# First batch's and left-over scores as F32 products of 64 rows, and a fixed order of the transition

## The chip, the cores and the metric

The kernel runs on one core of one Trainium2 chip. The metric is device time in microseconds (us) of one execution, the median of several runs. Engines: TensorE (PE: matmuls; PEld: its weight loads), VectorE (DVE), ScalarE (ACT), GpSimd (POOL), SyncE (SP, which here only issues DMAs). Every engine works through its own list in order and waits at semaphores.

## The reference, cut to what matters

Three layers on 2304 tokens: attention that keeps each query's 32 best scores, a two-layer MLP with a gate, and a layer in which each token goes to one of eight experts.

```python
# attention: B, H, S, D = 4, 8, 576, 64
scores = scale * np.matmul(q, k.transpose(0, 1, 3, 2))
kth = np.partition(scores, -32, axis=-1)[..., -32:-31]
scores = np.where(scores >= kth, scores, -1e9)
attn = softmax(scores)
x = np.matmul(attn, v)                          # -> (2304, 512)
# first MLP: w_in (512, 2048), w_out (2048, 512)
h = x @ w_in
x = (h * np.clip(h + 3.0, 0.0, 6.0) / 6.0) @ w_out
# routed layer: 8 experts, w1 (512, 1024), w2 (1024, 512)
logits = (x / norm(x)) @ (emb / norm(emb)).T / tau
e = argmax(logits); gate_w = softmax(logits)[e]
out = gate_w * (np.maximum(x @ w1[e], 0.0) @ w2[e])
```

## The kernel before, in words

**Numbers.** Matmuls run on F32 data in two ways. An F32R product takes a rounded operand in one pass; to keep the precision, each operand is split in a high part (a cast on ScalarE) and a low part (a subtraction on GpSimd or VectorE), and three products, or two with stacked operands, are summed. A plain F32 product needs no split and becomes two TensorE instructions.

**Units and steps.** The attention is cut into 72 units, 18 for each of the four batches. A tile unit ("t", b, t, p) is 128 queries of a pair of heads; with 576 keys each head gives a 128 x 576 block of scores. 576 is four tiles of 128 and 64 left over, so a left-over unit ("r", b, p) takes the last 64 queries of two pairs of heads, four heads in all. The order in a batch is tiles 0 and 1 (four units each), one left-over unit, tile 2, the other left-over unit, tile 3; in the last batch both left-over units stand behind tile 1.

The units pass through a software pipeline: in step i (76 of them) unit i gets its scores (`scores`, L397, in two halves g of 288 keys, each copied out by `take`, L400) and `pairs` (L409 to L413, VectorE, larger and smaller of two halves), unit i-1 its 32 maxima (`select`, L428 and L431, VectorE), unit i-2 the mask (`relu`, L442, ScalarE, and `mask`, L446, GpSimd), unit i-3 the exponential (L452) and the scaling by the inverse sum, unit i-4 its transposes (`turned`, L479, copied by `keep`, L484) and the product with v (`values`, L497, F32, left and right column halves in turn).

**Splitting q and k.** `prep` (L373) casts q, `need_k` (L322, L323) casts k twice, `lows` (L381) subtracts on GpSimd, and `ship` (L331) copies between partition halves by DMA, so that K holds the high and the low part of one head on 128 rows. A tile unit's half is then four F32R instructions (two heads, high and low q). A left-over unit's q goes into `zq`, a tile filled with zeros but for its columns, and its half is eight F32R instructions, summed onto one 128-row block.

**Work beside the attention.** In the same steps the first MLP's weights are prepared: 32 pieces are loaded (`w_load`, L220), turned from float64 words by VectorE (`w_one` L231, `w_two` L238), ScalarE (`w_round` L246, `w_hi` L259) and GpSimd (`w_add` L251, `w_low` L263), and their low parts are stored to DRAM (`w_store`, L267, lo_dram). They go through `wf`, a tile with three buffers. From step 12 the MLP runs too: an item is an eighth of the hidden width for 256 tokens, `s1` (L568, 24 instructions into bank_h), `gate` (L576), `swish` (L580), `large` (L584), `small` (L587), and one step later `s2` (L603, two halves). The steps in `PAUSE` start no item. `embed` computes the norms of the expert embeddings in five parts after steps 11, 12, 13, 14 and 16; part 2 is a product (L166) into a half of bank_a, which `values` uses as well, and part 3 a square root (L169).

**Order.** In the steps every engine's order is written out by hand: the names in FIRST (steps 0 to 11), MID (12 to 20) and THEN (21 on) are called one after another, and an engine gets its instructions in that order. Behind the steps a planner orders instructions by priority and estimated times; there the rest of the MLP runs, the last two groups of 128 tokens (left-over queries, groups 16 and 17) come last, `route` computes their logits, `choose` and `rank` the expert and the place of each token, `place` (L693) writes the token's number into a table. `ahead` has by then loaded the expert with the most tokens and its first two blocks of tokens; `stage1` (L963) and `stage2` (L976) are the expert's two matmuls, `tokens` (L812, L816) gathers and transposes rows, `split1` and `split2` (L796, L797) split weights.

## Time and profile before

| | before |
|---|---|
| median of 3 runs | 1116.71 us (1112.76 to 1118.89) |
| profiled execution | 1116.48 us |
| its span, first to last instruction | 1114.8 us |
| PE busy | 983.8 us, 88% |
| DVE busy | 775.3 us, 70% |
| ACT busy | 727.1 us, 65% |
| POOL busy | 646.6 us, 58% |
| mean granted clock of TensorE | 0.956 |

Busy time of TensorE counts an instruction from its start to the modelled end of its result, and instructions overlap; what one adds to a stream is the distance to the next start. The granted clock is the share of 2.4 GHz that TensorE was given; 0.5 would be 1.2 GHz throughout.

### The profile page before, as it was taken

To read this page: it belongs to the slowest core of one execution; us is meant where nothing else is said; L and a number is where in the kernel's file an instruction comes from. 1 tells how busy PE (TensorE), PEld (TensorE's weight loads), DVE (VectorE), ACT (ScalarE), POOL (GpSimd) and SP (SyncE) were. 2 spreads that over 40 slices of the span, in tenths; PEclk is the share of its full clock that TensorE was granted. 3 is DMA by queue.
4 is the path that set the end of the run, shared out by engine and by line. 5 is a ranking of instruction groups with operands and counts; after the bars stand their busy time and mean duration, and the time that the engine had idled before them with its cause. 6 is when DMAs were issued, how large, how long until landed. Compare 5 with 4: busy or idle time off the path is not lost.

```text
span 1114.8 us, 20782 instructions
## 1 busy us (share of the span) xinstructions
PE 983.8 (88%) x7172; PEld 861.7 (77%) x7172; DVE 775.3 (70%) x2345; ACT 727.1 (65%) x1469; POOL 646.6 (58%) x815
## 2 busy tenths in 40 slices
PE   2566658799999999999999999999989799999994
PEld 1345556689989789989788979889978688887883
DVE  4999878988898988898998799511244345444540
ACT  4798859888787878788887788632335244435541
POOL 5789868886676886677896677723221442113200
PEclk9967888899999999999999999999999899999997
DMA  6545656655334555343555324447680654345540
GB/s 185 170 148 168 215 186 199 206 186 189 115 116 130 148 172 190 113 133 115 158 183 170 126 73 142 126 160 206 188 283 23 195 195 157 130 168 173 196 163 20
DMA packets 90225, 176.11 MB, mean 158 GB/s; under 512 B 20477, under 2 KB 38032, under 8 KB 90111
## 3 DMA queue, kind: packets, MB, share of 16 engines
q1 hardware_dynamic: 85695, 164.90, 46.7%
q0 software_dynamic: 4416, 9.80, 2.6%
q8 instruction: 58, 0.95, 0.4%
q14 instruction: 56, 0.46, 0.1%
HBM read 150.86 MB, written 19.41 MB: 153 GB/s over the span
## 4 chain that ended last, share of the span: by engine, by line
PE 66%; DVE 12%; issue 7%; DMA 6%; ACT 5%; POOL 2%; SPq 1%; POOLq 0%; DVEq 0%; ACTq 0%
PE bank_h L568 17%; PE y L603 15%; PE ph L963 8%; PE po L976 7%; PE bank_a L497 6%; PE ps_sc L397 5%; PE bank_t L479 5%; DVE A L428 3%; DVE left L431 2%; DMA xg<-y_dram,idt 1%; DMA a<-in_moe_w_dram 1%; PE bank_t L640 1%; DVE wf L238 1%; DVE wf L231 1%; DMA lo_dram<-wf 1%
## 5 line engine op out<-in xcount | busy, mean ns | idle before, releaser
L446 POOL TENSOR_TENSOR s<-s,z 128x576 f32<-128x576 f32 x144 | 188.5, 1310 | 32.6 <-ACT z L442 31.2
L568 PE MATMUL bank_h<-xh,vh 128*128 128x256 f32 x576 | 170.7, 296 | 1.1 <-DVE u L580 1.1
L568 PE MATMUL bank_h<-xl,vh 128*128 128x256 f32 x576 | 164.5, 286 | 2.2 <-DVE xl L524 2.2
L568 PE MATMUL bank_h<-xh,lo 128*128 128x256 f32 x576 | 164.4, 285 | 0.0
L428 DVE MAX8 A<-left 128x8 f32<-128x288 f32 (+1 forms) x288 | 159.9, 597 | 0.0
L587 POOL TENSOR_TENSOR gl<-u,gh 128x512 fp32r<-128x512 f32 x72 | 94.6, 1314 | 93.0 <-ACT gh L584 91.9
L479 PE MATMUL bank_t<-ident,s 128*128 128x128 f32 x648 | 104.8, 288 | 35.9 <-ACT pt L484 30.9
L397 PE MATMUL ps_sc<-kst,qh 128*128 128x288 f32 x256 | 87.8, 356 | 44.9 <-DVE left L413 21.2
L580 DVE SCALAR_TENSOR_TENSOR u<-u,bank_h 128x512 f32<-128x512 f32 x72 | 49.3, 684 | 101.3 <-ACT u L576 99.8
L603 PE MATMUL y<-wh,gh 128*128 128x512 f32 x288 | 115.3, 402 | 0.0
L797 DVE TENSOR_TENSOR l<-a,h 128x1024 fp32r<-128x1024 f32 x64 | 77.9, 1242 | 53.5 <-ACT h L796 53.3
L479 PEld LDWEIGHTS bank_t<-ident,s 128*128 128x128 f32 x648 | 73.2, 145 | 54.0 <-ACT pt L484 36.0
L568 PEld LDWEIGHTS bank_h<-xh,vh 128*128 128x128 f32 x576 | 112.0, 195 | 3.0 <-DVE u L580 1.3
L568 PEld LDWEIGHTS bank_h<-xl,vh 128*128 128x128 f32 x576 | 112.1, 195 | 2.8 <-DVE xl L524 2.4
L603 PE MATMUL y<-lo,gh 128*128 128x512 f32 x288 | 113.2, 393 | 0.6 <-DMA lo<-lo_dram 0.6
L603 PE MATMUL y<-wh,gl 128*128 128x512 f32 x288 | 111.5, 391 | 2.5 <-POOL gl L587 2.5
L442 ACT ACTIVATE z<-s,nb 128x576 bf16<-128x576 f32 x144 | 111.8, 778 | 2.0 <-POOL nb L436 2.0
L452 ACT ACTIVATE s<-s,nb 128x576 f32<-128x576 f32 x144 | 112.3, 781 | 0.7 <-POOL s L446 0.6
L568 PEld LDWEIGHTS bank_h<-xh,lo 128*128 128x128 f32 x576 | 111.8, 194 | 0.1
L400 ACT COPY s<-ps_sc 128x576 f32<-128x576 f32 x144 | 92.4, 642 | 29.5 <-PE ps_sc L397 26.4
L497 PE MATMUL bank_a<-pt,vt 128*64 128x128 f32 (+1 forms) x1600 | 107.6, 289 | 0.7 <-DVE pos L678 0.7
L497 PEld LDWEIGHTS bank_a<-pt,vt 128*64 128x64 f32 x1600 | 89.7, 152 | 23.3 <-issue 8.0
(229 smaller groups left out, 2674.5 us busy)
## 6 DMA issues: line engine op xcount, KB each, us to landing
lo<-lo_dram SPq DMA_DIRECT2D x144, 512.0 KB, 4.1
a<-in_moe_w_dram SPq DMA_DIRECT2D x64, 512.0 KB, 9.9
qraw<-in_q_dram SPq DMA_DIRECT2D x64, 128.0 KB, 3.0
w<-in_moe_w_in_dram SPq DMA_DIRECT2D x16, 512.0 KB, 4.6
lo_dram<-wf SPq DMA_DIRECT2D x32, 256.0 KB, 2.8
w<-in_moe_w_out_dram SPq DMA_DIRECT2D x16, 512.0 KB, 4.7
vt<-in_v_dram SPq DMA_DIRECT2D x16, 320.0 KB, 3.2
kraw<-in_k_dram SPq DMA_DIRECT2D x32, 144.0 KB, 2.8
```

Of the source, the lines that this page charges most:

```text
L397: nc.tensor.matmul(ps[:, n, :HS], t, kk[:, HS * g:HS * g + HS], start=(o == 0), stop=(o == len(parts) - 1))
L400: nc.scalar.copy(sbuf[i % NS][:, :, HS * g:HS * g + HS], ps_[i][:, :, :HS])
L428: nc.vector.max(A[:, n, 8 * r:8 * r + 8], src[:, n, :w])
L442: nc.scalar.activation(zb_[n], tile_of(i, n), AF.Relu, bias=sel[i][1][:, n, 1:2], scale=-BIG)
L446: nc.gpsimd.tensor_tensor(s, s, zb_[n], op=ALU.subtract)
L452: nc.scalar.activation(s, s, AF.Exp, bias=sel[i][1][:, n, 0:1], scale=SCALE, accum_out=sums[i][:, n:n + 1])
L479: nc.tensor.transpose(pp[:, 128 * k:128 * k + 128], e[:, 128 * (3 * c + k):128 * (3 * c + k) + 128], ident)
L497: nc.tensor.matmul(av[64 * n:64 * n + 64, c0:c1], vt[:, k, 64 * n:64 * n + 64], pt[:, k + 5 * n if k < 4 else 4, c0:c1], start=(o == 0), s ...
L568: nc.tensor.matmul(ph[:, a, :], w, x[:, k, :], start=(k == 0 and n == 0), stop=(k == 3 and n == 2))
L587: nc.gpsimd.tensor_tensor(state[q][1], state.pop((q, "u")).rearrange("p (a n) -> p a n", a=2), state[q][0].bitcast(F32), op=ALU.subtract)
L603: nc.tensor.matmul(state["y"][o], x[:, a, c], w, start=(f == 0 and n == 0), stop=(f == 15 and n == 2))
L963: nc.tensor.matmul(ph, l[:, k, 128 * f:128 * f + 128], x[:, k, c0:c1], start=(n == 0), stop=(n == 11))
```

## The change

- `plain(u)` is true for every left-over unit and for the tile units of the first batch (PLAIN = 1). Such units keep q and k as loaded: no cast, no subtraction, no `ship`. Their scores are F32 products of 64 rows: head 0 on rows 0 to 63, head 1 on rows 64 to 127, and for a left-over unit each of two pairs of heads on 64 columns as well. `zq` and its zeros go. The first batch's k stays in the pool of the split k, the left-over units of later batches load k again.
- The last batch's units stand in the order of the others; PAUSE ends with 67, 71 instead of 66, 67.
- The lists FIRST, MID and THEN are new.
- `wf` has four buffers; the left-over units' output goes through it.
- `embed` follows steps 4 to 8, and its product goes to bank_h.
- The first loads: q of unit 0 is issued by ScalarE's queue, and the first weight piece is loaded right behind k.
- The end of the MLP: the last s2, the logits of groups 16 and 17, `choose`, `rank`, `stage1` of the first 256 tokens and `split2` of the first expert stand in a fixed order; the second expert's first weights are loaded ahead of them.

```diff
-PAUSE = (13, 17, 31, 35, 49, 53, 66, 67)
+PLAIN = 1
+PAUSE = (13, 17, 31, 35, 49, 53, 67, 71)
-FIRST = ("hi0 turn0 bend0 keep0 turn1 pick0 lows ship turn2 bend1 keep1 keep2 expo0 expo1 pick1 one0 round1 s10 hi1 s20 s21 score0 "
-         "low0 load_k values take0 load_q two0 mask0 guard round0 inverse s11 store0 pick2 pick3 mask1 gate aside low1 xh score1 "
-         "scale swish take1 large prep one1 two1 add0 bounds small add1 xl load0 load1 pairs store1 need_v")
+FIRST = ("turn0 hi0 pick0 need_v keep0 turn1 one0 expo0 low0 s10 keep1 turn2 hi1 keep2 lows s20 store0 expo1 round0 round1 s11 "
+         "load_q gate two0 guard ship one1 score0 pick1 load_k bend0 swish take0 values add0 load0 two1 inverse xh low1 scale "
+         "pick2 mask0 large score1 xl add1 small take1 pick3 pairs prep s21 store1 bend1 load1 bounds aside mask1")
-MID = ("lows s10 round0 expo0 hi0 turn0 turn1 one0 expo1 s11 gate two0 s20 pick0 low0 pick1 guard s21 bend0 ship keep0 score0 "
-       "load_k store0 keep1 turn2 add0 hi1 swish one1 take0 mask0 keep2 load_q inverse score1 large values round1 two1 take1 "
-       "pick2 aside bend1 load0 scale xh pick3 low1 small add1 mask1 need_v pairs xl prep load1 store1 bounds")
+MID = ("turn0 round0 lows keep0 s10 turn1 expo0 s11 load_q ship hi0 low0 turn2 expo1 score0 bend0 guard one0 gate load_k hi1 "
+       "pick0 two0 keep1 store0 s20 one1 pick1 mask0 add0 keep2 take0 two1 values bend1 inverse round1 pick2 add1 scale swish "
+       "load0 score1 low1 xh load1 store1 mask1 pick3 xl take1 bounds aside need_v large pairs prep small s21")
-THEN = ("lows turn0 pick0 expo0 keep0 turn1 expo1 s10 s11 ship bend0 turn2 score0 keep1 pick1 guard gate take0 keep2 inverse "
-        "mask0 swish scale large aside bend1 pick2 load_k s20 pick3 score1 take1 s21 values small prep mask1 pairs place xh "
-        "bounds load_q xl need_v")
+THEN = ("turn0 pick0 turn1 expo0 keep0 lows s10 s11 load_q expo1 guard keep1 pick1 turn2 ship score0 load_k bend0 gate mask0 "
+        "take0 keep2 inverse swish large scale small aside bend1 place pick2 s20 pick3 score1 take1 prep pairs s21 mask1 bounds "
+        "values xh xl need_v")
...
-            emb["pe"] = pe = half_a()
+            emb["pe"] = pe = bank_h
...
-        e["both"] = mp.tile([128, DM], F32, tag="wf", name="wf", bufs=3)
+        e["both"] = mp.tile([128, DM], F32, tag="wf", name="wf", bufs=4)
...
-        first, last = (r[1:], []) if b < B - 1 else ([], r[1:])
-        units += t[0] + t[1] + r[:1] + last + t[2] + first + t[3]
+        units += t[0] + t[1] + r[:1] + t[2] + r[1:] + t[3]
...
+    def plain(u):
+        return u[0] == "r" or u[1] < PLAIN
+
     def load_k(i):
-        if i >= NU or units[i][0] != "t":
+        if i >= NU:
+            return
+        if units[i][0] == "r":
+            _, b, p = units[i]
+            for a in range(2):
+                if b < PLAIN:
+                    rest_k[i, a] = kraws[b, p + a]
+                else:
+                    rest_k[i, a] = raw = lp.tile([128, S], F32, tag="kraw", name="kraw", bufs=2)
+                    for n in range(2):
+                        nc.sync.dma_start(out=raw[64 * n:64 * n + 64, :], in_=kt[b * H + 2 * (p + a) + n][64 * n:64 * n + 64, :])
             return
...
-            kraws[b, p] = raw = lp.tile([128, S], F32, tag="kraw", name="kraw", bufs=2)
+            if b < PLAIN:
+                kraws[b, p] = raw = kp.tile([128, S], F32, tag="k", name="kpl")
+            else:
+                kraws[b, p] = raw = lp.tile([128, S], F32, tag="kraw", name="kraw", bufs=2)
...
+        if plain(u):
+            w = 128 if u[0] == "t" else 64
+            for a in range(128 // w):
+                kk = kraws[u[1], u[3]] if u[0] == "t" else rest_k[i, a]
+                for n in range(2):
+                    d = slice(64 * n, 64 * n + 64)
+                    nc.tensor.matmul(ps[w * a:w * a + w, n, :HS], Q[u][d, w * a:w * a + w], kk[d, HS * g:HS * g + HS], start=True, stop=True)
+            return
         for n in range(2):
-            if u[0] == "t":
-                parts = [(K[u[1], 2 * u[3] + n], 128 * n)]
-            else:
-                parts = [(K[u[1], 2 * (u[2] + a) + n], 256 * n + 64 * a) for a in range(2)]
-            parts = [(kk, t[:, c:c + 128]) for kk, c in parts for t in Q[u]]
-            for o, (kk, t) in enumerate(parts):
-                nc.tensor.matmul(ps[:, n, :HS], t, kk[:, HS * g:HS * g + HS], start=(o == 0), stop=(o == len(parts) - 1))
+            for o, t in enumerate(Q[u]):
+                nc.tensor.matmul(ps[:, n, :HS], t[:, 128 * n:128 * n + 128], K[u[1], 2 * u[3] + n][:, HS * g:HS * g + HS], start=(o == 0), stop=(o == 1))
...
-        if i in (11, 12, 13, 14, 16):
-            embed((11, 12, 13, 14, 16).index(i))
+        if i in (4, 5, 6, 7, 8):
+            embed((4, 5, 6, 7, 8).index(i))
...
             load_k(0)
-            load_q(0)
+            load_q(0, nc.scalar)
+            w_load(0)
+            load_k(1)
             load_q(1)
-            prep(0)
-            lows()
-            load_k(1)
-            ship()
             load_q(2)
-            w_load(0)
-            prep(1)
-            lows()
...
-        while moe or last or side:
+        while moe or side:
...
+        with tc.manual_schedule():
+            for o in range(2):
+                last[6](last[0], o)
...
+            load1(1)
+            yts = []
+            for o, (t, g) in enumerate(finals):
+                pp = pps()
+                for k in range(4):
+                    nc.tensor.transpose(pp[:, k, :], t[:, 128 * k:128 * k + 128], ident)
+                yts.append(gp.tile([128, 4, 128], F32, tag="ob", name="ytl"))
+                nc.scalar.copy(yts[o], pp)
+                stage1(0, 0, 256, (o,))
+            for o, (t, g) in enumerate(finals):
+                p2 = half_a()[:, :E]
+                for k in range(4):
+                    nc.tensor.matmul(p2, yts[o][:, k, :], ent[:, k, :], start=(k == 0), stop=(k == 3))
+                nc.vector.tensor_copy(l_all[:, g, :], p2)
+                scored[0] += 1
+            choose()
+            for t, g in finals:
+                sq = gp.tile([128, DM], F32, tag="ob", name="sql")
+                nc.scalar.activation(sq, t, AF.Square, accum_out=ss_all[:, g:g + 1])
+            stage1(0, 0, 256, (2, 3))
+            rank()
+            stage1(0, 0, 256, (4,))
+            split2(0, range(5, 8), lambda f: stage1(0, 0, 256, (f,)))
         with tc.high_priority(offset=500):
-            stage1(0, 0, 256)
-        split2(0)
+            while spots:
+                place()
```

## Rows read from the trace of the kernel before

**Rows 1.** The page's slices of the span, 40 equal ones, busy tenths.

```profile
PE   2566658799999999999999999999989799999994
DVE  4999878988898988898998799511244345444540
```

**Rows 2.** Stages: length, busy us (instructions) per engine, granted clock, DMA share, GB/s.

```profile
28.00:112.00 84.00, 50.98 (x285) 38.91 (x285) 83.10 (x255) 72.53 (x148) 71.09 (x79) 0.80 0.52 161
112.00:224.00 112.00, 80.77 (x588) 69.20 (x588) 97.61 (x282) 91.42 (x185) 91.12 (x96) 0.83 0.64 202
224.00:700.00 476.00, 465.38 (x3878) 414.79 (x3876) 421.97 (x1479) 383.85 (x834) 353.71 (x500) 1.00 0.46 145
840.00:896.00 56.00, 47.09 (x297) 41.39 (x296) 23.77 (x64) 22.59 (x41) 18.63 (x20) 0.91 0.37 116
```

**Rows 3.** Timeline of the start (start, length, instruction), and the page's row for K's loads.

```profile
0.80 1.21 SPq L315 DMA_DIRECT2D kraw<-in_k_dram  x2
9.51 0.49 SPq L220 DMA_DIRECT2D w<-in_moe_w_in_dram  x1
10.16 0.58 PE L397 MATMUL ps_sc<-kst,qh 128*128 128x288 f32 x1 [10.16 <-DMA kst<-kraw]
11.73 0.64 ACT L400 COPY s<-ps_sc 128x576 f32<-128x576 f32 x1 [3.93 <-PE ps_sc L397]
14.18 0.43 DVE L231 TENSOR_SCALAR wf<-w 128x512 int32<-128x512 int32 x1 [13.24 <-DMA w<-in_moe_w_in_dram]
15.41 0.47 DVE L409 TENSOR_TENSOR ps_sc<-ps_sc,s 128x288 f32<-128x288 f32 x1
...
kraw<-in_k_dram SPq DMA_DIRECT2D x32, 144.0 KB, 2.8
```

**Rows 4.** Timeline of TensorE in a step at full clock.

```profile
299.84 1.31 PE L497 MATMUL bank_a<-pt,vt 128*64 128x128 f32 x20
301.08 0.88 PE L479 MATMUL bank_t<-ident,s 128*128 128x128 f32 x6
301.71 0.36 PE L568 MATMUL bank_h<-xh,vh 128*128 128x256 f32 x1
...
305.27 0.30 PE L397 MATMUL ps_sc<-kst,qh 128*128 128x288 f32 x1
305.40 0.29 PE L397 MATMUL ps_sc<-kst,ql 128*128 128x288 f32 x1
```

**Rows 5.** VectorE's waits from 100 to 226 us: total us, times, longest.

```profile
DVE wf L231 <- DMA lo_dram<-wf: 6.6, 4, 2.4
DVE u L580 <- ACT u L576: 5.2, 2, 5.0
```

**Rows 6.** Timeline around the norms' product.

```profile
151.25 1.85 PE L166 MATMUL bank_a<-sq,onesf 128*128 128x8 f32 x8 [8.85 <-DVE xl L524]
158.42 0.69 ACT L576 ACTIVATE u<-bank_h,half 128x512 f32<-128x512 f32 x1 [9.03 <-PE bank_h L568]
166.08 1.28 ACT L169 ACT_TABLE_LOAD   x1
```

**Rows 7.** The transition: timeline lines, and two lines of the chain (start, us, what).

```profile
844.42 0.40 PE L603 MATMUL y<-wh,gl 128*128 128x512 f32 x1
861.12 0.17 DVE L682 CAST rows<-de 128x2 int32<-128x2 f32 x1
874.30 1.11 PE L816 MATMUL pxt<-ident,xg 128*128 128x128 f32 x4 [5.44 <-DMA xg<-y_dram,idt]
877.36 0.90 PE L816 MATMUL pxt<-ident,xg 96*128 96x96 f32 x4 [1.94 <-DMA xg<-y_dram,idt]
878.83 0.77 PE L963 MATMUL ph<-xh__10004,h 128*128 128x224 f32 x2 [0.57 <-ACT xh__10004 L817]
...
850.10 2.84 PE ph L963 x24
878.83 5.32 PE ph L963 x24
```

**Rows 8.** One line of the code by its instructions: duration ns min/median/max.

```profile
L231 DVE TENSOR_SCALAR wf<-w x32: 409/553/1443, 14.2 to 207.1; 128x512 int32<-128x512 int32 x32
```

More of the change, by code (lines that the diff above doesn't have):

```diff
@@ L295, in layers @@
     sbuf = [wk.tile([128, 2, S], F32, name=f"s{i}") for i in range(NS)]
-    zq = [wk.tile([128, 448], F32R, name=f"zq{i}") for i in range(2)]
     left = wk.tile([128, 2, S], F32, name="left")
@@ L627, in r1 @@
         def r1():
-            sq = mp.tile([128, DM], F32, tag="wf", name="sqy", bufs=3)
+            sq = mp.tile([128, DM], F32, tag="wf", name="sqy", bufs=4)
             nc.scalar.activation(sq, ysb, AF.Square, accum_out=ss_all[:, g:g + 1])
@@ L834, in ahead @@
         load2(0)
+        expert(1)
     def step(i, last):
@@ L887, in layers @@
     if True:
-        for t in zq:
-            nc.gpsimd.memset(t.bitcast(F32), 0.0)
         last = None
@@ L928, in layers, with split2 @@
                 finish_rest()
-        if "w1" not in late:
-            at.close()
-            ahead()
-        assert done_groups[0] == NG and "order" in late
-        st.close()
-        hp = mb.enter_context(tc.tile_pool(name="hp", bufs=1))
-        tk = mb.enter_context(tc.tile_pool(name="tk", bufs=1))
-        wb = mb.enter_context(tc.tile_pool(name="wb", bufs=1))
-        gp = mb.enter_context(tc.tile_pool(name="gp", bufs=3))
-        px = mb.enter_context(tc.tile_pool(name="px", bufs=2, space=PSUM))
-        po_ = mb.enter_context(tc.tile_pool(name="po_", bufs=3, space=PSUM))
+        assert "w1" in late and done_groups[0] == NG - 2
         hs = {}
-        def split2(r):
+        def split2(r, then=(), f=None):
+            then = deque(then)
             a2 = ws2[r]
@@ L949, in split2, with stage1 @@
                 split(h2[:, k:k + 2, :], l2[:, k:k + 2, :], a2[:, k:k + 2, :])
+                if then:
+                    f(then.popleft())
             ws2[r] = (h2, l2)
-        def stage1(r, c0, c1):
+        def stage1(r, c0, c1, fs_=range(8)):
             xh_, xl_ = tok[r]
@@ L957, in stage1 @@
             hh, hl = hs[r]
-            for f in range(8):
+            for f in fs_:
                 ph = late["ph"].tile([128, 512], F32, tag="ph", name="ph2")[:, :c1 - c0]
@@ L1011, in layers @@
         nc.tensor.transpose(pg[:NG, :128], gt, ident)
-        gts = fs.tile([NG, 128], F32, tag="gts", name="gts")
+        gts = fs.tile([NG, 128], F32, tag="df", name="gts")
         nc.vector.tensor_copy(gts, pg[:NG, :128])
@@ L1021, in layers @@
             if then is not None:
-                load1(then)
+                if r:
+                    load1(then)
                 load2(then)
```

88 lines of the change are left out of this document (49 added, 39 removed).

## The prediction

> **What bounds the kernel now.** I read the slices of the span first, then the same stages with sums, then each stage's waits. The slices show three regimes [rows 1]: VectorE at nine tenths while TensorE climbs (to about 224 us), TensorE at nine tenths to the end, and a dip of TensorE near 820 to 880 us. The stage table [rows 2] prices them: from 28 to 112 us VectorE is busy 83.10 of 84 us and TensorE only 50.98 at a granted clock of 0.80; from 112 to 224 VectorE has 97.61 of 112, so 14.4 us are idle, with ScalarE at 91.42 and GpSimd at 91.12 close behind; from 224 to 700 TensorE has 465.38 of 476 at full clock. So a microsecond is worth something in four places: before VectorE's first work, in VectorE's idle time of 112 to 224, in TensorE's work behind 224, and in the dip. Elsewhere ScalarE and GpSimd work comes and goes free.
>
> The sums are made against the profiled execution, 1116.5 us (span 1114.8 and 1.7 around it); the median of the runs shown is 1116.7, the same within 0.02%.
>
> **The start.** Before, step 0's scores need q and k split into two parts: two ScalarE casts of K, GpSimd subtractions and a copy between partition halves, and the first product starts at 10.16 us. Its result is copied at 11.73, but VectorE gets its first work only at 14.18, when the first weight piece lands, issued at 9.51, 4.67 us earlier; the scores' pairs follow at 15.41 [rows 3]. After, K and q go straight to TensorE, q through ScalarE's own queue, which is idle then. SyncE issues K's two halves from 0.80 for 1.21 us; 2.8 us from issue to landing gives about 4.8. The first score part takes some 1.4 us at the half clock (twice the 0.7 us worked out below): 6.2. The weight piece is issued third, at 2.0, and lands at 6.7. ScalarE's rounding of it stands ahead of the copy (about 0.7), the copy takes 0.64 as at 11.73 [rows 3]: 8.0. Second part and copy, with 0.2 of passing on: 10.3. Pairs at 10.4 instead of 15.41: **-5.0**, and as VectorE then has no idle time up to 112 us, all of it carries. Bounds: -2 if the copies queue, -6 if the weight piece lands early.
>
> **Steps 1 to 11.** In these steps VectorE's own list is the same: the first batch's units lose GpSimd subtractions, ScalarE casts and copies on SyncE, all hidden behind VectorE. One thing can leak: the 409 ns weight shift L231 has a median of 553 and a maximum of 1443 ns [rows 8], beside GpSimd work in the profile. Fewer subtractions and another order change these meetings; an excess of 144 ns by the median, times the 19 pieces of these steps, is 2.7 us, and I take about half, **-1.5** (bounds -6 and +4: the order was rewritten and can meet worse).
>
> The scores themselves get dearer. A plain F32 product goes as two instructions: L497's 800 products are 1600 instructions. Twenty of them take 1.24 us, 62 ns each for 128 columns, with left and right column halves in turn; six F32 transposes take 0.63 us, 105 ns for 128 columns in one block [rows 4]. That is 0.48 or 0.82 ns per column, and an F32 product of 288 columns costs 0.28 or 0.47 us. An F32R instruction of 288 columns has a pitch of 0.13 [rows 4]. A tile unit's part goes from 4 x 0.13 = 0.52 to two products, 0.56 to 0.95; I take 0.7, near L497's row, since the two heads lie in different rows of the array but only the second half of one product can meet the first of the next. A left-over unit's part goes from 8 x 0.13 = 1.04 to 1.11 to 1.89; I take 1.2. No row here shows a product of 64 rows, so the lower ends reach down to four blocks at once, 0.47. At the half clock all of these double; the scores' way (two parts, two copies) is then 2 x (1.4 + 0.64) plus about 1.5 of waits, 5.6 us, inside the 7 to 8 us in which VectorE picks maxima between two units' pairs. Cost 0 here; if the cover goes, see the third rival.
>
> The Trainium skill, TensorEngine Tiling (Array Packing), Theoretical Speedup, says that a contraction of at most 64 rows can run up to twice as fast by row tiles; by that the parts would be 0.47 and, with columns halved too, 0.24. In Key Properties it says against the change that "changing tiling mode (not just tile) drains the TensorE". With 0.1 us a drain as an estimate, two per part, 12 parts in full steps would add 1.2 us. No row here shows either for row halves.
>
> **Steps 12 to 21.** Of VectorE's 14.4 idle us, two waits hold 11.8 [rows 5]. The first, 6.6 us, is L231 waiting for a store to lo_dram: three `wf` buffers turn over too fast; a fourth comes in, and store0 moves ahead of the next step's need. The second, 5.2, is `swish` behind `gate`: ScalarE stood 9.03 us for bank_h because TensorE stood 8.85 us at the norms' product L166, which had taken a half of bank_a that L524 had still to read [rows 6]. The product moves to step 6 and to bank_h, unused there; the wait has no successor. The square root's table load, 1.28 us, and the one back also leave a stage where ScalarE is full for step 7, where VectorE covers them. What is late next: with VectorE packed, 97.6 us of its work faces 91 on ScalarE and GpSimd (which lose some 1 us a step of casts and subtractions) and TensorE's 80.77 at a clock of 0.83. I take two thirds of 11.8, -7.9, and give back 0.9 for five tile units' parts (5 x 2 x 0.18, half on the path): **-7.0**. Bounds: -13 and +3, the latter if the new order makes waits as large as it removes.
>
> **From step 22.** The list THEN keeps TensorE's order word for word (turn, s1, turn2, score0, s20, score1, s21, values); only ScalarE's bend0 and the loads of K and q move, and q and K come earlier. So tile units cost the same. The left-over units at steps 26, 44 and 62 stand in full steps: 3 x 2 x 0.16 = +1.0; those at 31, 49 and 67 are in pauses, where TensorE has room. In the last batch one such unit moves from a full step to a pause: -2 x 0.52 = -1.0. Sum **0**, bounds -4.4 and +4.1 (six parts at 0.47 or at 1.89, with the same -1.0). The left-over units' K loads (four issues each) go to SyncE two steps ahead of use; behind them stand only loads with a step or more to spare.
>
> **The transition.** Before, the second layer's last matmul starts at 844.42; the places (`rows`) are known at 861.12, 16.5 us after its end; the gathered tokens reach TensorE at 874.30 after 5.44 us of idling, the next after 1.94 more, and 24 instructions of 224 columns then take 5.32 us, while 24 of 256 columns had taken 2.84 [rows 7]. The stage's clock is 0.91 [rows 2]. Idle 5.44 + 1.94 + 0.57 (the wait before 878.83) and 2.7 of half clock: 10.7 us to win. After, `rank` has a fixed place behind four blocks of stage1 (half of 2.84 each, 5.7) and the transposes and logits of two tiles, about 3: 9.5 us instead of 16.5, so tokens come 7 us earlier, and the same filling (rest of stage1, first stage2 blocks) covers them. Against it: the planner had put 2.6 us of stage1 into waits ahead of 844, which the fixed order keeps behind. **-8.0**, bounds 0 and -12.
>
> **Sum**: -5.0 - 1.5 - 7.0 + 0 - 8.0 = -21.5, so 1116.5 - 21.5 = **1095.0**.
>
> **Rivals.** (a) The freed waits return elsewhere: in 112 to 224 the three engines are within 7% of each other, so packing one shows the next; and the fixed transition only trades idle places. Then the start, a third of the middle and a third of the transition remain: -5.0 - 2.3 - 2.7 = -10, 1106.5. For it: the near-equal sums. Against it: L166's stall is one instruction's and has no substitute. (b) Nothing to be measured: the start's gain is eaten by left-over products that run one after another (+4.1) and the middle is even: 1115. (c) Slower: F32 products run one after another, 1.9 us a tile part at the half clock, and the scores' way, 2 x (1.9 + 0.64) + 1.5 = 6.6, plus any queueing on ScalarE passes the 7 to 8 us between pairs. It decides once a copy queues over 1 us. Each of 11 steps then loses about 2 us and each of six in the middle 1.5: +31; with +4.1 behind, -5.0 at the start, and a transition of -8.0: 1138. For it: ScalarE's list now puts copies behind casts of weights. Against it: TensorE busy only 50.98 of 84. (d) Products in different row halves run wholly at once: six left-over parts at 0.47 instead of 1.2, -4.4, and ten tile parts in the middle at 0.47 instead of 0.7, half of them on the path, -1.2: 1089.4. For it: L497's column halves come near two at once [rows 4]. Against it: the two instructions of one product follow each other in one block. It is the two-fold rule of the Trainium skill, TensorEngine Tiling (Array Packing), Theoretical Speedup.
>
> **How the numbers follow.** Forecast 0.50, (a) 0.22, (b) 0.08, (c) 0.10, (d) 0.10. About 0.5%, 5.6 us, is what a measurement of this kernel can tell from no change; the bounds are 1110.9 and 1122.1. Faster: the forecast and (d), all but 0.01, and nine tenths of (a): 0.79. Same: (b) and the rest: 0.10; slower: (c) with a little of (b): 0.11. The range reaches from the sum with the better ends of start, middle and transition (another -1, -6 and -4: 1084) and a part of (d)'s -5.6, to past (a) and (b): 1080 to 1117. It leaves out (c) and about as much at the low end.
>
> **What would show it.** Right: VectorE's first pairs near 10.4 us; no L231 wait on lo_dram and no L166 stall; a clock above 0.83 in the middle; steps from 22 on at the same pace; xg's transposes without a wait of several microseconds. Wrong: idle VectorE between 28 and 112 (scores late), ScalarE or GpSimd releasing VectorE for 10 us in the middle, score parts of 1.9 us at full clock, or `rank` still 16 us behind the last y.

## The result, and the profile after

The changed kernel takes 1087.99 us (median of 4 runs, 1084.72 to 1092.13), the kernel before 1117.8 beside it: ratio 0.9743, 95% interval 0.9695 to 0.9791. A second set of 5 runs gave 1091.64 and 0.9738 (0.9707 to 0.9769). The forecast was 1095.0. The execution profiled took 1086.53 us, its span is 1084.8.

The sum can be laid out by marks that both traces share: the first instruction on VectorE that works on a unit's scores (its pairs), and TensorE's last matmul of the first MLP (the last y).

| us | before | after | difference | forecast |
|---|---|---|---|---|
| first pairs of unit 0 | 15.41 | 10.08 | -5.33 | -5.0 |
| unit 0 to unit 11 | 107.54 | 103.85 | -3.69 | -1.5 |
| unit 11 to unit 21 | 119.04 | 104.37 | -14.67 | -7.0 |
| unit 21 to unit 71 | 459.63 | 459.41 | -0.22 | 0 |
| unit 71 to the last y | 142.80 | 138.71 | -4.09 | (transition) |
| last y to the end of the span | 270.34 | 268.34 | -2.00 | -8.0 |

So -23.7 us come before unit 21, ten more than forecast, and the rest, -6.3, behind it. The -8.0 was forecast for the transition as a whole, the last two rows together. The page's slices (PE and DVE, busy tenths of 40 equal parts) answer to [rows 1]: the same three regimes, the first one ending a slice earlier.

```profile
PE   3666777999999999999999999999989998999994
DVE  6999999888889988889988889411234353445540
```

The stage table (length, busy us with instructions per engine in the order PE, PEld, DVE, ACT, POOL, then granted clock, DMA share, GB/s) answers to [rows 2]. From 112 to 224 us VectorE is now busy 106.31 of 112 instead of 97.61, ScalarE and GpSimd 99 instead of 91, and TensorE's clock is 0.92 instead of 0.83: the stage is packed more densely, by all engines at once.

```profile
28.00:112.00 84.00, 57.46 (x322) 36.60 (x323) 82.32 (x273) 76.20 (x154) 67.22 (x76) 0.72 0.49 161
112.00:224.00 112.00, 93.30 (x732) 75.62 (x731) 106.31 (x330) 99.35 (x204) 99.76 (x118) 0.92 0.69 224
224.00:700.00 476.00, 464.34 (x3910) 405.50 (x3908) 413.89 (x1443) 377.33 (x819) 347.77 (x483) 1.00 0.50 147
840.00:896.00 56.00, 53.32 (x322) 46.24 (x321) 25.07 (x36) 23.79 (x39) 23.25 (x23) 1.00 0.51 174
```

The timeline of the start (start, length, instruction, and in brackets the idle time before it with what ended it) answers to [rows 3]. Products start at 3.87 instead of 10.16, the weight piece lands for VectorE at 6.80 (6.7 forecast), the second copy runs at 9.41, the pairs follow at 10.08 (10.4 forecast).

```profile
3.87 2.64 PE L411 MATMUL ps_sc<-kpl,qpl 64*128 64x288 f32 x4 [3.87 <-DMA qpl<-in_q_dram]
...
6.80 0.43 DVE L232 TENSOR_SCALAR wf<-w 128x512 int32<-128x512 int32 x1 [5.87 <-DMA w<-in_moe_w_in_dram]
...
9.41 0.64 ACT L418 COPY s<-ps_sc 128x576 f32<-128x576 f32 x1 [1.43 <-PE ps_sc L411]
10.08 0.47 DVE L427 TENSOR_TENSOR ps_sc<-ps_sc,s 128x288 f32<-128x288 f32 x1 [2.13 <-ACT s L418]
```

VectorE's waits from 112 to 224 us (total, times, longest) answer to [rows 5]. Both waits of before are gone, and none over 1.3 us has come.

```profile
DVE ps_sc L427 <- ACT s L418: 2.5, 3, 1.3
DVE sums L477 <- POOL sums L474: 1.7, 2, 1.2
DVE u L598 <- ACT u L594: 1.0, 1, 1.0
```

The same by marks, from unit 11's pairs to unit 21's, first before, then after, in the columns of the stage table: VectorE's busy time (the third engine) goes from 102.95 to 99.73 us. Its waits of more than 0.15 us in this stretch go from 15.4 to 4.2.

```profile
122.95:241.99 119.04, 91.64 (x678) 79.41 (x680) 102.95 (x309) 96.61 (x196) 97.23 (x114) 0.87 0.62 194
113.93:218.30 104.37, 85.67 (x662) 68.17 (x662) 99.73 (x305) 93.53 (x191) 93.70 (x111) 0.92 0.68 217
```

The transition, answering to [rows 7]: `rows` is written 13.07 us behind the start of the last y instead of 16.70, and TensorE's waits for gathered tokens there are 0.90 and 1.45 us instead of 5.44 and 1.94.

```profile
816.42 0.39 PE L621 MATMUL y<-wh,gl 128*128 128x512 f32 x1
829.49 0.17 DVE L706 CAST rows<-de 128x2 int32<-128x2 f32 x1
842.24 0.63 PE L843 MATMUL pxt<-ident,xg 128*128 128x128 f32 x4 [0.90 <-DMA xg<-y_dram,idt]
844.89 0.52 PE L843 MATMUL pxt<-ident,xg 96*128 96x96 f32 x4 [1.45 <-DMA xg<-y_dram,idt]
```

### The profile page after: what moved, and what is told of

Read it like the earlier page. It is cut to its first block, busy times and chain, and to the rows that moved or that the text cites. A ratio compares the mean times of both kernels' runs of the same rounds, so it can differ in the third digit from the quotient of the medians.

```text
span 1084.8 us, 20732 instructions
## 1 busy us (share of the span) xinstructions
PE 979.7 (90%) x7172; PEld 833.9 (77%) x7172; DVE 763.1 (70%) x2345; ACT 714.1 (66%) x1437; POOL 619.5 (57%) x785
## 5 line engine op out<-in xcount | busy, mean ns | idle before, releaser
L464 POOL TENSOR_TENSOR s<-s,z 128x576 f32<-128x576 f32 x144 | 185.7, 1290 | 43.4 <-ACT z L460 42.0
L621 PE MATMUL y<-wh,gh 128*128 128x512 f32 x288 | 118.0, 410 | 0.0
L515 PEld LDWEIGHTS bank_a<-pt,vt 128*64 128x64 f32 x1600 | 87.2, 147 | 39.3 <-ACT pt L502 15.5
L515 PE MATMUL bank_a<-pt,vt 128*64 128x128 f32 (+1 forms) x1600 | 104.8, 284 | 11.2 <-ACT pt L502 9.9
L418 ACT COPY s<-ps_sc 128x576 f32<-128x576 f32 x144 | 92.2, 641 | 23.1 <-PE ps_sc L411 11.6
L502 ACT COPY pt<-bank_t 128x384 f32<-128x384 f32 x216 | 101.6, 476 | 0.5 <-PE bank_t L497 0.5
```

What stands on the lines that cost most here:

```text
L418: nc.scalar.copy(sbuf[i % NS][:, :, HS * g:HS * g + HS], ps_[i][:, :, :HS])
L464: nc.gpsimd.tensor_tensor(s, s, zb_[n], op=ALU.subtract)
L502: nc.scalar.copy(pts[i][:, 3 * c:3 * c + 3, :].rearrange("p k n -> p (k n)"), tb_.pop((i, c))[:, :384])
L515: nc.tensor.matmul(av[64 * n:64 * n + 64, c0:c1], vt[:, k, 64 * n:64 * n + 64], pt[:, k + 5 * n if k < 4 else 4, c0:c1], start=(o == 0), s ...
L621: nc.tensor.matmul(state["y"][o], x[:, a, c], w, start=(f == 0 and n == 0), stop=(f == 15 and n == 2))
```

## The experiments

Theory after the result: the gain before unit 21 is made of three parts that each free VectorE (the norms moved, a fourth `wf` buffer, products that leave GpSimd and ScalarE lighter, together with the new lists), and the fixed transition gives the rest. Rivals: one part alone carries it; or the transition's gain is from elsewhere. All times are compared with the kernel before on the same chip. The stretch behind the last y turned out to differ by up to 15 us between executions of one and the same kernel, so the table also gives the start of the last y, which is free of it. Where a mark is compared with after's below, it is with the mean of after and after_again (103.2, 105.0 and 816.8). The marks have a spread of their own: after, after_again, old_tail, xg3, load1_late and old_tail_xg3 have the same steps, and their profiles give 102.3 to 103.9, 102.6 to 105.7 and 812.7 to 817.2. The kernel before has one profile.

| kernel | median us | ratio (95%) | unit 0 to 11 | 11 to 21 | last y at | last y to end |
|---|---|---|---|---|---|---|
| before | 1117.8 | 1 | 107.5 | 119.0 | 844.4 | 270.3 |
| after | 1088.0 | 0.9743 (0.9695 to 0.9791) | 103.9 | 104.4 | 816.4 | 268.3 |
| after_again | 1091.6 | 0.9738 (0.9707 to 0.9769) | 102.5 | 105.7 | 817.2 | 283.3 |
| norms_back | 1093.6 | 0.9777 (0.9746 to 0.9809) | 99.4 | 108.6 | 814.2 | 279.5 |
| wf3 | 1114.7 | 0.9969 (0.9951 to 0.9988) | 109.9 | 115.6 | 835.2 | 274.5 |
| old_lists | 1105.8 | 0.9887 (0.9855 to 0.9919) | 110.6 | 108.1 | 826.7 | 277.1 |
| split_first | 1109.9 | 0.9924 (0.9899 to 0.9948) | 108.8 | 105.6 | 830.4 | 279.3 |
| same_rows | 1103.3 | 0.9861 (0.9828 to 0.9893) | 108.0 | 106.7 | 822.7 | 278.7 |
| old_tail | 1090.1 | 0.9745 (0.9713 to 0.9777) | 102.4 | 104.4 | 815.8 | 272.4 |
| before_norms | 1112.9 | 0.9947 (0.9929 to 0.9965) | 110.5 | 112.2 | 840.6 | 269.6 |
| before_norms_wf4 | 1109.7 | 0.9923 (0.9897 to 0.9949) | 110.7 | 106.8 | 835.9 | 272.4 |
| xg3 | 1089.1 | 0.9747 (0.9704 to 0.9790) | 102.3 | 104.7 | 814.6 | 269.3 |
| load1_late | 1093.4 | 0.9793 (0.9765 to 0.9822) | 102.7 | 102.6 | 812.7 | 273.0 |
| old_tail_xg3 | 1091.5 | 0.9767 (0.9743 to 0.9790) | 102.5 | 104.5 | 816.7 | 274.3 |

**The norms (norms_back, before_norms).** The one puts them back in the changed kernel, the other moves them in the kernel before.

```diff
 # norms_back
-            emb["pe"] = pe = bank_h
+            emb["pe"] = pe = half_a()
...
-        if i in (4, 5, 6, 7, 8):
-            embed((4, 5, 6, 7, 8).index(i))
+        if i in (11, 12, 13, 14, 16):
+            embed((11, 12, 13, 14, 16).index(i))
```

> The changed kernel with the norms of the expert embeddings back after steps 11, 12, 13, 14 and 16 and their product in a half of bank_a. If the stall of the product was worth what the prediction gave it (5.2 us of VectorE's waits, and the two table loads back among the full steps), steps 12 to 21 take 4 to 7 us more and the whole about 1093 us. If the new lists read that half of bank_a early enough (the product with v now stands before swish), no stall comes back and only the table loads cost: 0 to 2 us, about 1089 us.

> The kernel before with one part of the change alone: the norms of the embeddings after steps 4 to 8, their product into bank_h. Theory (my prediction's: the product's stall of 2.3 us and the square root's wait in the middle stood on VectorE's path, and the earlier steps have room): steps 11 to 21 shorten by 2 to 4 us, steps 0 to 11 grow by less than 2, the time is 1113 to 1117 against 1118. Rival (from the run with the norms back at steps 11 to 16 under the new lists, where steps 0 to 11 were 4.4 us shorter and 11 to 21 4.3 longer: the norms cost about 4 us wherever they stand): steps 0 to 11 grow by 4, 11 to 21 shrink by 4, no change in time within 2 us.

In the kernel before, the move takes 6.9 us out of units 11 to 21 and puts 3.0 into 0 to 11; the last y comes 3.8 earlier and the ratio is 0.9947. The middle wins more than the 4 us that either expectation allowed, and the steps ahead lose more than the theory's 2. So this part was undervalued in the middle (its wait is 5.2) and not free ahead of it: VectorE, the full engine there, does the norms' own three instructions, 2.2 us in before_norms. In the changed kernel no gain of the move can be told, though the middle answers nearly as the first expectation has it: 0 to 11 loses 3.8, 11 to 21 wins 3.6, the last y, 2.7 later than in norms_back, lies within the spread, and the intervals of the two ratios overlap. The reason stands in the trace of norms_back: under the new lists the product waits 1.06 us at its old place, where it had waited 8.85 [rows 6].

```profile
132.53 1.03 PE L167 MATMUL bank_a<-sq,onesf 128*128 128x8 f32 x8 [1.06 <-DVE xl L542]
```

**The fourth buffer (wf3, before_norms_wf4).**

```diff
 # wf3: wf with three buffers, xq in a tile of its own
-        e["both"] = mp.tile([128, DM], F32, tag="wf", name="wf", bufs=4)
+        e["both"] = mp.tile([128, DM], F32, tag="wf", name="wf", bufs=3)
...
-            xq = mp.tile([128, DM], F32, tag="wf", name="xq", bufs=4)[:, :128].rearrange("d (a t) -> d a t", a=2)
+            xq = mp.tile([128, 2, 64], F32, tag="xq", name="xq", bufs=1)
```

> The changed kernel with three wf buffers instead of four, and the left-over output in a tile of its own as before. If the stores to lo_dram were the wait and the fourth buffer removed it, VectorE's L232 waits for them again and steps 5 to 21 take 4 to 7 us more: about 1093 us. If the new lists' earlier store is what removed it, nothing moves: 1087 to 1089 us.

> The kernel before with two parts of the change: the norms after steps 4 to 8 and the fourth buffer of wf (with the left-over units' output through it). The norms alone gave 1112.93 against 1119.06. In the changed kernel taking the fourth buffer away cost some 23 us. Theory (the buffer pays only together with the new lists and the lighter ScalarE and GpSimd, since the old lists were laid out for three): steps 0 to 21 are 0 to 6 us shorter than with the norms alone, 1107 to 1113. Rival (the buffer is worth its 23 us by itself, and is most of the change): 1090 to 1096.

Without the buffer the changed kernel loses nearly all, far more than the 4 to 7 us expected: the last y is 18.4 us later. VectorE's waits from 28 to 240 us name the store to lo_dram for 14.9 of them; for one more wait of the same tile, 5.2, the profile names nothing.

```profile
DVE wf L232 <- DMA lo_dram<-wf: 14.9, 10, 5.7
DVE wf L232 <- issue: 5.2, 1, 5.2
```

Put into the kernel before beside the norms, the buffer takes another 5.4 us out of units 11 to 21, within the 0 to 6 expected: the first row below, VectorE's waits of before_norms from 112 to 240 us, is missing in before_norms_wf4 (second fence), where none is longer than 1.2.

```profile
DVE wf L231 <- DMA lo_dram<-wf: 8.1, 3, 3.9
DVE ps_sc L409 <- ACT s L400: 1.2, 1, 1.2
```

```profile
DVE u L580 <- ACT u L576: 1.5, 3, 0.9
DVE ps_sc L409 <- ACT s L400: 1.2, 1, 1.2
```

So norms and buffer together bring units 11 to 21 from 119.0 to 106.8 with the old lists and the split products, 12.3 of the 14.7 us that the middle won. By the marks the buffer is worth 5 us under the old lists (the intervals of these two ratios overlap) and 18 under the new ones; why so much more there, no run shows.

**The lists and the unsplit first batch (old_lists, split_first).** old_lists is the changed kernel with FIRST, MID and THEN of before; split_first has

```diff
-PLAIN = 1
+PLAIN = 0
```

and the order of the first loads and casts of before.

> The changed kernel with the three lists FIRST, MID and THEN of the kernel before, all else as changed. If the gain of steps 1 to 21 (18.4 us between the pairs of unit 0 and of unit 21) comes from the removed waits and the removed casts and subtractions, most of it stays: about 1092 us, steps 12 to 21 at 106 to 110 us. If it comes from the order itself, steps 12 to 21 go back towards 115 us and the whole to 1100 us or more.

> The changed kernel with PLAIN = 0: the first batch's tile units are split again (casts, subtractions, copies between halves, four F32R instructions a part, and the old first loads); the left-over units stay plain. By the prediction the start gives back 5 us and steps 1 to 21 about 2 us: about 1095 us. If the casts and subtractions that fell away were what let ScalarE and GpSimd keep up in steps 12 to 21 (8 us more gained there than forecast), these steps give back 5 us or more beyond the start: about 1100 us.

split_first costs more than either time expected. old_lists comes out at the second of its two (1100 or more), but not by the middle, which is 3.1 us longer there and 0.6 in split_first. split_first gives back 7.1 us at the start (first pairs at 17.64). In units 0 to 11 old_lists loses 7.4 and split_first 5.6 us, where VectorE's list of work is the same and its waits are small (at most 2.5 us in sum behind the first pairs). What differs is how long two of its instructions take. The rows are VectorE's groups from unit 0's pairs to unit 11's (busy us, mean ns, idle before), first the kernel before, then after, old_lists and split_first:

```profile
L231 DVE TENSOR_SCALAR wf<-w 128x512 int32<-128x512 int32 x18 | 14.3, 794 | 0.0
L238 DVE SCALAR_TENSOR_TENSOR wf<-w,wf 128x512 int32<-128x512 int32 x18 | 13.6, 756 | 0.6
```

```profile
L239 DVE SCALAR_TENSOR_TENSOR wf<-w,wf 128x512 int32<-128x512 int32 x18 | 13.2, 732 | 0.4
L232 DVE TENSOR_SCALAR wf<-w 128x512 int32<-128x512 int32 x18 | 7.5, 419 | 1.4 <-DMA w<-in_moe_w_in_dram 1.4
```

```profile
L239 DVE SCALAR_TENSOR_TENSOR wf<-w,wf 128x512 int32<-128x512 int32 x18 | 16.4, 913 | 0.6
L232 DVE TENSOR_SCALAR wf<-w 128x512 int32<-128x512 int32 x18 | 12.8, 711 | 0.0
```

```profile
L239 DVE SCALAR_TENSOR_TENSOR wf<-w,wf 128x512 int32<-128x512 int32 x18 | 16.3, 904 | 0.4
L232 DVE TENSOR_SCALAR wf<-w 128x512 int32<-128x512 int32 x18 | 9.2, 511 | 1.6 <-DMA w<-in_moe_w_out_dram 1.6
```

The shift of a weight piece takes 419 ns on the mean after and 794 before, 18 times: 6.8 us. Both instructions together are 8.5 us longer in old_lists than after, and 4.8 in split_first. A long one stands beside a GpSimd instruction that had begun before it, and ends 0.3 us after that one has ended, as here before (VectorE's shift, then GpSimd's mask, which ends at 39.35; the shift ends at 39.64):

```profile
38.20 1.44 DVE L231 TENSOR_SCALAR wf<-w 128x512 int32<-128x512 int32 x1
...
38.07 1.28 POOL L446 TENSOR_TENSOR s<-s,z 128x576 f32<-128x576 f32 x1
```

Of the 32 shifts of before, the 14 longest, 920 to 1443 ns, all stand so and end 0.28 to 0.29 us behind it; the four with no GpSimd instruction beside them take 420 to 427. So it is a wait inside the instruction, and no view of waits shows it. The Trainium skill, SBUF — State Buffer (Who interferes with whom), says that a tensor_scalar can run in a mode that uses the pair of ports which VectorE shares with GpSimd, and that the engine that issues first holds the pair for its whole instruction; the traces agree, with the lengths above. Under the new lists none of the 18 shifts begins with more than 0.16 us of a GpSimd instruction still to run, and they take 410 to 434 ns; with the split products GpSimd has 12 instructions more in the same eleven units (96 against 84), and shifts up to 877 ns are back. That both are needed follows from the two runs: before_norms needs 110.5 us for these units, before_norms_wf4 110.7 and after 103.2, and with either undone all or most of these 7 us are back.

**Products side by side (same_rows).** The first batch's two heads both stand on rows 0 to 63, q in two column ranges and k in two tiles; its left-over units load k again. Of the edit, the products:

```diff
+        if plain(u) and u[0] == "t":
+            for n in range(2):
+                nc.tensor.matmul(ps[:, n, :HS], Q[u][0:64, 128 * n:128 * n + 128], kraws[u[1], u[3]][n][0:64, HS * g:HS * g + HS], start=True, stop=True)
+            return
         if plain(u):
```

> The first batch's two heads both stand on rows 0 to 63 (q in two column ranges, k in two tiles, the same bytes and scores), so their two F32 products share one block of rows and cannot run side by side. Theory (the two products of a tile part overlap because they stand in different row halves): a tile part takes 0.95 to 1.0 us at full clock instead of 0.69, and about 1.9 instead of 1.3 at the lower clock. Over steps 0 to 20 with 16 units of two parts that is 32 x 0.3 to 0.6 = 10 to 19 us of TensorE time; since VectorE and the copies set the pace there, I expect 0 to 4 us of it in the kernel's time (1088 to 1092), most of it at the first pairs (+1). Rival (c) of the prediction, that the scores' way decides when the products run one after another: +20 or more, first in steps 0 to 11, with waits of VectorE's pairs for ScalarE's copies.

TensorE's timeline at full clock, first after, then same_rows: a tile unit's part lasts 0.69 us to the next instruction's start in the one and 1.17 in the other; at the lower clock it is 1.26 (38.57 to 39.83) and 2.18 (38.78 to 40.96).

```profile
148.97 0.76 PE L411 MATMUL ps_sc<-kpl,qpl 64*128 64x288 f32 x4
149.66 0.50 PE L621 MATMUL y<-wh,gh 128*128 128x512 f32 x1
...
264.01 0.39 PE L621 MATMUL y<-lo,gh 128*128 128x512 f32 x1
264.24 0.39 PE L621 MATMUL y<-wh,gl 128*128 128x512 f32 x1
264.56 0.72 PE L411 MATMUL ps_sc<-kraw,qpl 64*64 64x288 f32 x8
265.21 0.50 PE L621 MATMUL y<-wh,gh 128*128 128x512 f32 x1
265.54 0.39 PE L621 MATMUL y<-lo,gh 128*128 128x512 f32 x1
265.77 0.40 PE L621 MATMUL y<-wh,gl 128*128 128x512 f32 x1
```

```profile
160.43 1.23 PE L406 MATMUL ps_sc<-kpl,qpl 64*128 64x288 f32 x4
161.60 0.50 PE L624 MATMUL y<-wh,gh 128*128 128x512 f32 x1
...
38.78 2.25 PE L406 MATMUL ps_sc<-kpl,qpl 64*128 64x288 f32 x4
40.96 0.48 PE L518 MATMUL bank_a<-pt,vt 128*64 128x128 f32 x2
```

So the two products of a part do run side by side. The lower rows of the first fence show a left-over unit's four products, on two halves of rows and of columns, in 0.65 us, less than two products need. In the raw starts all four blocks' first instructions begin within 0.02 us, and the second ones 0.29 later. The same rows show what the change of blocks costs: y's products start 0.23 us apart, the scores 0.32 behind one, and the first y product behind the scores takes 0.33 to the next start. That is some 0.1 us each way. Taking the side-by-side products away puts the last y 5.9 us later, more than the 0 to 4 expected and far from rival (c)'s 20, although TensorE's granted clock rose: 0.94 instead of 0.77 between unit 0 and unit 11, with TensorE busy 84.4 us instead of 64.9. VectorE's waits for copies of scores are 1.9 us there instead of 0.2 (without the one ahead of the first pairs), and 5.9 instead of 2.5 between units 11 and 21. The median is 11.6 us above after_again's; some 6 of them aren't in the marks, and behind the last y nothing was edited.

**The end of the MLP (old_tail, after_again).** old_tail is the changed kernel with the planner's end:

```diff
-            final = gs[o] >= NG - 2
+            final = False
...
-        while moe or side:
+        while moe or last or side:
...
-            load1(1)
-            yts = []
...
-            rank()
-            stage1(0, 0, 256, (4,))
-            split2(0, range(5, 8), lambda f: stage1(0, 0, 256, (f,)))
```

> The changed kernel with the end of the MLP as before: the planner orders the last logits, choose, rank, stage1 and split2, and the second expert's first weights are loaded late. Theory (the fixed order is what shortened the stretch behind step 71): rows are written about 16 us behind the last y instead of 13, the time is 4 to 8 us longer, 1092 to 1096. Rival (the stretch behind step 71 is shorter for another reason, such as the emptier queue of MLP items, and the fixed order only trades one wait for another): within 2 us of the changed kernel, 1087 to 1090.

> The changed kernel itself, once more, beside three others on one chip. The four experiments before it all ended with 274.5 to 279.5 us from the last y to the end, against 268.3 in the changed kernel's profile, with the same instructions in the same order on every engine there. If that is a cost of their edits, this run shows 268 to 270 and a time near 1088. If it differs from one execution to the next, by when the gathered rows arrive, this run may show 272 to 280 as well, and the four times then carry up to 10 us that are not their edits'.

The theory fell: 0.9745 against 0.9738 on the same chip. In old_tail `rows` is 16.91 us behind the last y, 3.84 later than after, as expected, and the waits for gathered tokens are back:

```profile
832.70 0.17 DVE L706 CAST rows<-de 128x2 int32<-128x2 f32 x1
...
846.30 1.12 PE L843 MATMUL pxt<-ident,xg 128*128 128x128 f32 x4 [5.86 <-DMA xg<-y_dram,idt]
850.26 0.90 PE L843 MATMUL pxt<-ident,xg 96*128 96x96 f32 x4 [2.84 <-DMA xg<-y_dram,idt]
```

But from `rows` to the end it needs 255.4 us, while the fixed order needs 255.3 in after and 270.4 in after_again. Over all profiles of the table the planner's order needs 252.9 to 257.3 us in five, the fixed order 255.3 to 270.4 in nine. So what the fixed order wins ahead of `rows` it gives back behind, in after itself least. The shorter stretch from unit 71 to the last y (138.79 in old_tail) isn't its doing either: 252 second-layer matmuls stand there before, 240 after and in old_tail, as the last batch's units and pauses were laid otherwise, and from unit 54 to unit 71 that batch takes 2.5 us longer for it.

**Where it is given back (xg3, load1_late, old_tail_xg3).**

```diff
 # xg3, and in old_tail_xg3 with old_tail's edits
-        pool("xg", bufs=2)
+        pool("xg", bufs=3)
 # load1_late: the second expert's first weights behind the table
-            load1(1)
             yts = []
...
         for r in TURNS[1:]:
             load_ids(r, 0, 4)
+        load1(1)
```

> The changed kernel with one more buffer for gathered rows of tokens (three instead of two). With the old, planner-ordered end the time was the same (1090.05 against 1091.64) although the rows were written 3.9 us later, so the fixed order's gain is given back behind them. Theory A: it is given back where TensorE waits for gathered rows (3.8 to 4.0 us about 100 us behind the last y in the executions of the fixed order, 0.5 to 1.1 in those of the planner's), since GpSimd issues these gathers only when TensorE has freed one of the two buffers. Then a third buffer takes 4 to 8 us off the stretch from the rows to the end (with the half clock that follows such a wait), and the time is 1082 to 1087. Theory B: the giving back has other causes (the second expert's weights, loaded 25 us earlier, beside the gathers): the wait stays or moves, within 2 us of the changed kernel, 1087 to 1092.

> The changed kernel with the second expert's first weights (2 MB) issued behind the rows' table, as in the kernel before, not ahead of the fixed order. Theory B: these loads stand beside the last y rows, the table and the first gathers, and move the later loads of weights too; without them there the stretch from the rows to the end is 253 to 256 us, as in the three executions of the planner's order, and the time is 1082 to 1087. Theory A (the buffers for gathered rows are what counts): within 2 us of the changed kernel, with the waits for gathered rows as they were, 1087 to 1092; a later load may even cost 1 to 3 us where its splitting stands on ScalarE's path.

> The planner-ordered end together with three buffers for gathered rows. Theory A: the planner's order waits for gathered rows 5.4 and 2.8 us ahead of the first expert's rest (about 24 and 31 us behind the last y), which is the latency from the table to the rows and not the buffers, so the third buffer gives 0 to 2 us: 1088 to 1091. Rival: any buffer shortens it, 1084 or less.

Theory A's wait is there in after and goes with the third buffer. These are TensorE's transposes of the next expert's rows, in after, then in xg3, where the four of 128 columns follow the four of 48 without a wait, then in old_tail, where the wait is 0.53 us with two buffers:

```profile
914.36 0.63 PE L843 MATMUL pxt<-ident,xg 128*128 128x128 f32 x4 [3.60 <-DMA xg<-y_dram,idt]
```

```profile
914.26 1.03 PE L843 MATMUL pxt<-ident,xg 48*128 48x48 f32 x8
```

```profile
918.28 0.63 PE L843 MATMUL pxt<-ident,xg 128*128 128x128 f32 x4 [0.53 <-DMA xg<-y_dram,idt]
```

Yet xg3's time is after's (0.9747), its runs from 1082.39 to 1097.44. In load1_late the wait is gone as well, with two buffers (the longest there is 0.84 us), against theory A's expectation that it stays; but the time (0.9793) is no lower, so theory B fell outright. So the wait can be taken away in two ways, and neither saves time that can be measured. old_tail_xg3 (0.9767) was within half a microsecond of theory A's range.

What remains is a stall that comes and goes, 45 to 65 us behind the last y. ScalarE's rows in after_again, then in xg3, show it: the second instruction follows 5.12 and 6.72 us of idling, put down to no engine ("remote").

```profile
863.90 0.59 ACT L844 CAST xh__10647<-pxt 128x512 fp32r<-128x512 f32 x1 [1.93 <-remote]
869.61 0.60 ACT L970 ACTIVATE hh<-ph 128x224 fp32r<-128x224 f32 x2 [5.12 <-remote]
```

```profile
860.59 0.36 ACT L970 ACTIVATE hh<-ph 128x224 fp32r<-128x224 f32 x1 [4.84 <-PE ph L968]
867.67 0.60 ACT L970 ACTIVATE hh<-ph 128x224 fp32r<-128x224 f32 x2 [6.72 <-remote]
```

The product that ScalarE waits for is in the trace: the last of its twelve starts at 865.28 in after_again and at 865.01 in xg3, and the semaphore that it raises comes at 869.58 and 867.64. In after the same product starts at 859.47, and its semaphore comes at 859.76. So TensorE itself stood still there (the profile models the ends of its matmuls and doesn't show it), in the same order of instructions that in after runs through. Idle time of 1.5 to 4.6 us in TensorE's rows at this place stands in most of the other profiles too, in three of the five of the planner's order among them, so it isn't shown to be the fixed order's. What held TensorE stays open, and so does where the transition's gain goes.

## Why the prediction came out near, point by point

**The start** held: 10.08 for 10.4. From the weight piece on each step is in its place (6.80 for 6.7). Ahead of it two misses cancel: the products began at 3.87 instead of 4.8, and the first part took 2.64 us instead of 1.4, as its second head's q landed later (two of its four instructions start at 3.87 and 4.51, the others at 5.18 and 5.82).

**Steps 1 to 11** had the right mechanism and the wrong size. The excess was priced by the median of the shift's length (144 ns over 409) and halved; the mean over these eleven units is 794, an excess of 375 that went entirely, 18 x 0.375 = 6.8 us. Against that stand some 3 us that the norms add there (before_norms), which the prediction had put behind VectorE's cover although VectorE is the full engine. VectorE's busy time between these marks went from 106.44 to 100.64 us; its waits went from none to 2.4 us in after and 1.0 in after_again.

**Steps 12 to 21** were the largest miss: -14.7 for -7.0. The two waits named were the right ones. Two steps failed. One is the discount to two thirds, out of respect for ScalarE and GpSimd at 91 of 112: they packed along with VectorE (99 of 112), and VectorE's waits fell by 11.2 us in all, where 7.9 were taken. The other is a term that the sum left out: VectorE's own work in the stage fell by 3.2 us, of which 2.0 are the norms' instructions. By experiments, the norms' move gave -6.9 where 5.2 of wait stood; the buffer gave -5.4, though the 8.1 us of waits on the store that stood there without it all went, as VectorE's instructions grew longer by 2.8 in sum; the difference to after, 2.4, is left for lists and products together.

**From step 22** the sum was right up to unit 71 (-0.2 for 0), its terms not. A left-over part costs 0.65 us, or 0.74 with the change of blocks ahead of it, instead of 1.2, for the prediction let the second instruction of one product hold up the next block's first; rival (d) had that right, though its 0.47 was not reached, and the tile part at 0.69 was forecast at 0.7 by a wrong mixture. The 0.1 us that the prediction's estimate puts on a change of blocks is what the rows show; its 1.2 us are 12 such changes, two for each of six parts, not 12 parts. And by its own figures the two-fold rule applied twice gives 0.47 for a left-over part, a quarter of 1.89, not 0.24. Some steps gained (from unit 25's pairs to unit 26's: 10.19 to 9.73 us), 2.7 us from unit 21 to unit 54, and the last batch, laid otherwise, gave 2.5 back. The 4.1 us from unit 71 to the last y were not in the sum: they stand in old_tail too, and so are not the transition's.

**The transition** failed. `rows` moved 3.6 us, not 7: it comes 13.07 us behind the last y for a forecast 9.5, whose own parts, 5.7 and 3, add up to 8.7, and 3 us of the way (824 to 827) ran at a granted clock of 0.51. In one profiled pair the stretch from unit 71 shrank by 6.1, but undoing the fixed order costs nothing that can be measured. The term should have been 0: the prediction followed the gain to the first gathered tokens and no further, and rival (a) had named the trading of idle places.

So the forecast of -21.5 was near the -30.0 partly by luck: 10.2 us too little before unit 21 and 4.3 too little from there to the last y stand against a transition that was put 6.0 too high by this pair and 8.0 by old_tail. Rival (a) fell in the middle, where 4.2 us of waits are left of 15.4, and rival (c) in the early steps: behind the first pairs VectorE waited 0.2 us for copies. Rival (b) fell with the time. Rival (d)'s 1089.4 is close to the time by chance, though its mechanism is the true one.

## What to carry to other kernels

Where an engine is full, look at the spread of its instructions' lengths, by the mean and not the median: a wait inside an instruction appears in no view of waits, and reordering the neighbour can take it out. Don't discount a wait on a stage's bound engine because the engines beside it are nearly as busy: here their shares of busy time rose along with it, and nearly the whole wait was won. Count the bound engine's own instructions that a move takes along, at both ends. And follow a gain at a transition to the end of the span, or to the next place where the engine is sure to wait, before it is counted.

## What the runs showed of the hardware

Plain F32 products in four blocks of 64 rows by 64 columns took 0.65 us for 288 columns each, two products in different row halves 0.69 and two in the same rows 1.16 to 1.17, all at full clock. A change from products on 128 rows and columns to such blocks and back took some 0.1 us each way (0.32 us between starts instead of 0.23, and 0.33 instead of 0.23). A 409 ns VectorE shift took up to 1443 ns beside a GpSimd instruction that had begun before it. A higher granted clock went with longer early steps: with products one after another TensorE was granted 0.94 instead of 0.77 there, and the steps took 108.0 us instead of 103.2; what the clock alone does to them, no run shows. Two executions of one instruction order differed by 15 us over 270 (268.3 and 283.3 behind the last y). A stall of TensorE of some 4 us is a part of it, with a granted clock of 0.58 in the 8 us behind it (870 to 878 in after_again); TensorE's whole granted clock from `rows` to the end was 0.94 instead of 0.97.
